# Zeros of the cache gradients: copied within memory from a first piece, in place of stores from a row on the chip

## The chip, the cores and the metric

The kernel runs on one core of a Trainium2 chip. The metric is the device time of one execution in microseconds (us); several executions are given by their median. A profile is one execution taken with the hardware profiler. Its span runs from the first to the last instruction; the execution's own time is a little longer.

## The reference

One token passes through two identical layers, each an attention over a window of a key/value cache followed by a dense block with the mish activation. The kernel returns the output and the gradients of all inputs.

```python
W = min(4096, max(256, Sk // 4))          # 4096 of Sk = 32768 positions
k = k_cache[:, :, Sk - W:, :]             # 4 groups of heads, 128 wide; v likewise
p = softmax(q @ k.T * Dh ** -0.5);  o = p @ v
x = x + attention(layernorm(x)) @ wo      # D = 1024, 32 heads
x = x + mish(layernorm(x) @ w1 + b1) @ w2 # F = 3584
# the same two lines once more with the same weights and caches;
# outputs: x and the vector-Jacobian product with grad_out
```

The gradients of the caches have the caches' full shape, (1, 4, 32768, 128) in bf16. Only the last 4096 positions took part, so the first 28,672 positions of each of the 4 groups of both caches have a gradient of zero. These zeros are 58.7 MB, and the kernel has to write them: about 60% of all that it writes.

## The kernel before, in words

The forward pass runs through attention, dense block, attention, dense block, and the backward pass returns through them in reverse. At the end come the weight gradients, which are outer products on TensorE.

Weights and cache windows are loaded by SyncE (SP) through `Ring` (L35 to L78), eight slots of 1 MB. `pump` (L68 issues the load) goes on in a fixed order as long as a slot is free, and `release` frees a slot once the work on it is queued. `W1`, `VS` and `KT` have places of their own. Attention weights pass through `EX`, the first half of `DSX`, and end in `PX` (first written at L530, in `attn_fwd`), which the backward pass reads at L805 and L958. The finished weight gradients and the window parts of the cache gradients leave through SP, too (`store`, L917), from stages that reuse `W1`, `VS`, `KT` and the ring.

The zeros are the filler of the schedule. A list, `zjobs`, holds 56 destinations of 1 MB: `out_2` and `out_3`, four groups each, seven pieces per group. A piece is 128 partitions by two rows of 4 KB (`ZC` = 2048 bf16). Each partition owns 224 rows of a cache group, 56 KB, so a piece is 128 stretches of 8 KB that lie 56 KB apart. All come from one tile of zeros, `zt`, 4 KB in each partition, which VectorE sets at the start (L168). `zeros(n, after)` (L237 to L243) first has GpSimd copy one element of `after` into `pz` (L238), so that GpSimd, which works in order, waits until that point of the computation. Then it issues the next `n` pieces from GpSimd's own DMA queue:

```python
nc.gpsimd.tensor_copy(pz[0:1, ...], after[0:1, 0:1])
...
nc.gpsimd.dma_start(dst, zt[:, None, :].to_broadcast([P, dst.shape[1], ZC]))
```

The calls are placed by hand: 6 pieces in the second attention's forward pass, 7 after it, 7 before the second dense block's backward pass, and then groups of 2 to 5 through the rest of the backward pass. GpSimd has little else to do: constants at the start, and small copies into `QC` (L470) and `DOC` (L785), whose second halves are read by TensorE late in the backward pass. ScalarE issues small DMAs, among them the three loads of inputs at the start (L196 to L198).

Of the kernel before, what the change touches and what calls it, by code (L numbers as in the profile page):

```python
# [10 lines left out]
BF16 = mybir.dt.bfloat16  # L11
# [4 lines left out]
P = 128  # L16
# [67 lines left out]
def kernel(  # L84
# [22 lines left out]
    nc = tc.nc  # L107
# [3 lines left out]
    ZR = Sk - W  # L111
# [7 lines left out]
    def sb(shape, dtype, name):  # L119
        return keep.tile(shape, dtype, name=name)  # L120
# [14 lines left out]
    PX = sb([P, 2 * 1024], BF16, "PX")  # L135
# [3 lines left out]
    gbc = DSX[:, 1024:2048]  # L139
    junk = sb([P, 1024], BF16, "junk")  # L140
    ZC = 2048
    zt = sb([P, ZC], BF16, "zt")


    SC = [psum.tile([P, 512], FP32, name=f"SC{i}")[:] for i in range(2)]
# [29 lines left out]
    for hi in range(4):  # L175
        r = slice(32 * hi, 32 * hi + 32)
# [47 lines left out]
    zjobs = []  # L224
    for out_t in (out_2, out_3):
        for g in range(G):
            dst = out_t[0, g, 0:ZR, :].rearrange("(p r) d -> p (r d)", p=P).rearrange("p (r c) -> p r c", c=ZC)
            for k in range(0, dst.shape[1], 2):
                zjobs.append(dst[:, k:k + 2, :])
    zjobs.reverse()  # L230

    pz = sb([1, 32], FP32, "pz")
    pz_n = [0]

    def zeros(n, after=None):

        if after is not None and zjobs:  # L237
            nc.gpsimd.tensor_copy(pz[0:1, pz_n[0]:pz_n[0] + 1], after[0:1, 0:1])  # L238
            pz_n[0] += 1
        for _ in range(n):  # L240
            if zjobs:
                dst = zjobs.pop()
                nc.gpsimd.dma_start(dst, zt[:, None, :].to_broadcast([P, dst.shape[1], ZC]))  # L243


    KEEP_Q = (6, 7)
# [452 lines left out]
    def wo_hook1(c):  # L699
        if c == 0:  # L700
            zeros(6, OC[:, 0, 1:2])
        conv(1)

    x3, st3, sA1 = attn_fwd(1, x2, st2, False, wo_hook1, last_da)
    zeros(7, x3)
    sB1 = mlp_fwd(1, x3, st3)
    conv(8, "A")
# [137 lines left out]
    nc.vector.tensor_tensor(out=dh1[:], in0=da1[:], in1=mp1[:], op=ALU.mult)  # L845
    nc.vector.tensor_copy(DHC[:, :, 1], dh1[:])
    zeros(7, dh1)
    g3 = dn_b1(g4)
    sB1["act_late"]()
# [224 lines left out]
```

## Time and profile before

| what | value |
|---|---|
| median of 3 runs | 479.27 us (478.96 to 480.3) |
| the profiled execution | 478.89 us, span 477.1 us |
| busy: TensorE, VectorE, ScalarE, GpSimd | 351.7, 277.9, 245.3, 45.2 us |
| moved by DMA | 183.41 MB, mean 384 GB/s |
| memory read, written | 83.90 MB, 98.58 MB |
| pieces of zeros | 56, issued from 137.5 to 378.0 us |
| from issue to landing of a piece | 4.8 / 13.0 / 24.5 us (least, median, most) |

A DMA is issued on the queue of an engine: q1 is SP's, q10 ScalarE's, q0 GpSimd's (`software_dynamic`), and q8 carries the fetches of instructions. All run on the same 16 DMA engines. A transfer is cut into packets, here one for each row. The share in the table of queues is the time that a queue's packets took, as a part of the 16 engines' time in that stretch; packets overlap slightly, so a full stretch reads a little over 100%. In a row of the stretches, "x" is the number of instructions. The chain of waits is followed back from the last instruction, at each step to what released it.

### The profile page before, as it was taken

The page shows a single profiled execution, that of the slowest core. Times are in us where ns is not written, and L with a number is a line of the kernel's source. Part 1 is how long each engine was busy: PE and PEld are TensorE (multiplying, and loading weights), DVE is VectorE, ACT ScalarE, POOL GpSimd, SP SyncE. Part 2 cuts the span into 40 slices and gives each one's busy share as a digit, 9 for nine tenths or more (in the row PEclk, how much of TensorE's full clock was granted, in tenths as well). Part 3 has the DMA queues.
Part 4 walks back from the last instruction along what each step waited for, and adds up shares of the span by engine and source line. Part 5 has one row for each costly group of instructions (what it writes and reads, how often), then busy time and mean ns, then how long its engine had stood idle before and what let it go on. Part 6 is the DMA issues. An engine that isn't in the chain of part 4 may idle for free.

```text
span 477.1 us, 13273 instructions
## 1 busy us (share of the span) xinstructions
PE 351.7 (74%) x5841; PEld 268.5 (56%) x5841; DVE 277.9 (58%) x597; ACT 245.3 (51%) x358; POOL 45.2 (9%) x83
## 2 busy tenths in 40 slices
PE   4846345696688895888886976688778689999930
PEld 3746335696588784877876975556456323333300
DVE  4405820561331268896598825466176889999920
ACT  2402001171145296792594633675267589999920
POOL 1000000000043130102201011002302200000000
PEclk9955555555555588797897555555555555555555
DMA  8999999999969999999999999678999999999997
GB/s 337 423 419 419 418 419 418 421 400 383 420 252 394 396 394 406 347 410 368 416 421 366 363 345 414 229 190 325 417 420 415 388 415 413 418 420 414 419 420 306
DMA packets 33992, 183.41 MB, mean 384 GB/s; under 512 B 4217, under 2 KB 4238, under 8 KB 20622
## 3 DMA queue, kind: packets, MB, share of 16 engines
q1 hardware_dynamic: 17280, 123.74, 64.5%
q0 software_dynamic: 15232, 58.72, 31.2%
q8 instruction: 45, 0.74, 0.6%
q10 hardware_dynamic: 1422, 0.10, 0.2%
q14 instruction: 13, 0.11, 0.1%
HBM read 83.90 MB, written 98.58 MB: 382 GB/s over the span
## 4 chain that ended last, share of the span: by engine, by line
PE 46%; DMA 19%; DVE 16%; issue 7%; ACT 6%; ACTq 2%; DVEq 0%; SPq 0%
DVE junk L399 10%; PE BIG L921 8%; PE BIG L421 8%; DMA ring<-in_A_wo_dram 6%; PE SC L921 5%; DMA ring<-in_A_wq_dram 4%; DMA W<-in_B_w_dram 4%; PE BIG L568 3%; ACT ring L282 3%; PE MV L634 3%; DMA out_dram<-W 3%; PE BIG L967 2%; PE TP L433 2%; PE MV L587 2%; ACTq L884 2%
## 5 line engine op out<-in xcount | busy, mean ns | idle before, releaser
L282 ACT COPY ring<-BIG 128x1024 bf16<-128x1024 bf16 x82 | 81.8, 1046 | 38.5 <-PE BIG L421 29.4
L399 DVE CUSTOM_DVE_ANT_0 junk<-ring,SC 128x1024 bf16<-128x1024 bf16 x62 | 75.5, 1217 | 6.1 <-PE SC L305 3.4
L421 PE MATMUL BIG<-ident_bf,ring 128*128 128x128 bf16 x656 | 71.0, 278 | 8.9 <-ACT ring L282 2.4
L921 PE MATMUL BIG<-W 2*128 2x512 bf16 x163 | 68.3, 586 | 7.5 <-ACT W L282 3.2
L421 PEld LDWEIGHTS <-ring 128*128 128x128 bf16 x656 | 57.4, 126 | 22.0 <-issue 21.0
L921 PEld LDWEIGHTS <-W 2*128 2x128 bf16 x240 | 20.2, 101 | 39.9 <-issue 35.3
L243 POOL DMA_DIRECT2D out_dram<-zt x56 | 40.2, 720 | 3.5 <-DMA out_dram<-zt 3.0
L282 ACT COPY KT<-BIG 128x1024 bf16<-128x1024 bf16 x22 | 21.8, 1015 | 31.5 <-PE BIG L568 29.6
L282 ACT CAST W<-BIG 128x512 bf16<-128x512 f32 x55 | 31.2, 595 | 11.5 <-PE BIG L921 9.3
L433 PEld LDWEIGHTS <-ring 128*128 128x128 bf16 x704 | 30.8, 107 | 11.2 <-ACT ring L282 6.3
L921 PE MATMUL SC<-W 2*128 2x512 bf16 x77 | 35.3, 584 | 0.4 <-ACT VS L282 0.4
L282 ACT COPY W<-BIG 128x1024 bf16<-128x1024 bf16 (+2 forms) x33 | 26.5, 908 | 17.2 <-PE BIG L727 14.8
L279 DVE CAST W<-BIG 128x512 bf16<-128x512 f32 x30 | 20.3, 686 | 20.8 <-PE BIG L921 13.4
L539 PE MATMUL MV<-OC,ring 128*128 128x1 bf16 x512 | 16.5, 166 | 13.0 <-DMA ring<-in_A_wo_dram 12.2
L587 PE MATMUL MV<-NB,W 128*128 128x1 bf16 x448 | 16.4, 172 | 10.0 <-DMA W<-in_B_w_dram 6.6
L539 PEld LDWEIGHTS <-ring 128*128 128x128 bf16 x512 | 15.9, 106 | 13.7 <-DMA ring<-in_A_wo_dram 12.8
L461 PE MATMUL MV<-NA,ring 128*128 128x1 bf16 x512 | 15.0, 165 | 10.6 <-DMA ring<-in_A_wq_dram 9.4
L399 DVE CUSTOM_DVE_ANT_0 junk<-ring,DSX 128x1024 bf16<-128x1024 bf16 x18 | 22.0, 1224 | 0.5
L587 PEld LDWEIGHTS <-W 128*128 128x128 bf16 x448 | 16.1, 118 | 10.7 <-DMA W<-in_B_w_dram 7.7
L399 DVE CUSTOM_DVE_ANT_0 junk<-ring,SC,dnp 128x1024 bf16<-128x1024 bf16 x16 | 20.5, 1281 | 0.6
L967 PEld LDWEIGHTS <-W 32*128 32x128 bf16 x128 | 9.6, 101 | 19.9 <-issue 18.3
L461 PEld LDWEIGHTS <-ring 128*128 128x128 bf16 x512 | 14.3, 103 | 11.2 <-DMA ring<-in_A_wq_dram 10.0
(253 smaller groups left out, 593.3 us busy)
## 6 DMA issues: line engine op xcount, KB each, us to landing
out_dram<-zt POOLq DMA_DIRECT2D x56, 1024.0 KB, 13.0
ring<-in_A_wq_dram SPq DMA_DIRECT2D x27, 1024.0 KB
ring<-in_A_wo_dram SPq DMA_DIRECT2D x24, 1024.0 KB
ring<-in_B_w_dram SPq DMA_DIRECT2D x14, 1024.0 KB
out_dram<-W SPq DMA_DIRECT2D x11, 1024.0 KB
W<-in_B_w_dram SPq DMA_DIRECT2D x8, 896.0 KB
out_dram<-KT SPq DMA_DIRECT2D x7, 1024.0 KB
out_dram<-ring SPq DMA_DIRECT2D x7, 1024.0 KB
```

What stands on the lines that cost most here:

```text
L243: nc.gpsimd.dma_start(dst, zt[:, None, :].to_broadcast([P, dst.shape[1], ZC]))
L279: nc.vector.tensor_copy(dst, src)
L282: nc.scalar.copy(dst, src)
L399: nc.vector.tensor_tensor_reduce(out=out, in0=a, in1=vec, scale=1.0, scalar=acc if i else 0.0, op0=ALU.mult, op1=ALU.add, accum_out=acc)
L421: nc.tensor.transpose(b[:, i * P:(i + 1) * P], block(w, i) if block else w[:, i * P:(i + 1) * P], ident_bf[:])
L433: nc.tensor.matmul(out, lhsT=w[:, i * P:(i + 1) * P], rhs=rhs_of(i), start=fresh[0], stop=last and i == n - 1, skip_group_check=True)
L461: nc.tensor.matmul(q_ps[:, h:h + 1], lhsT=ch[:, h * P:(h + 1) * P], rhs=NA[:, t, l:l + 1], start=(t == 0 and h == 0), stop=(t == TD - 1), ...
L539: nc.tensor.matmul(y_ps[:, dd:dd + 1], lhsT=ch[:, tt, dd * P:(dd + 1) * P], rhs=OC[:, h, l:l + 1], start=(h == 0 and dd == 0), stop=(h == ...
L568: nc.tensor.transpose(b[:, i * P:(i + 1) * P], T[:, g, 8 * b8 + i, :], ident_bf[:])
L587: nc.tensor.matmul(h_ps[:, fb:fb + 1], lhsT=f_block(W1[:, t], fb), rhs=NB[:, t, l:l + 1], start=(t == 0 and fb == 0), stop=(t == TD - 1), ...
L921: nc.tensor.matmul(b[:, 0:n], lhsT=ROWS[base:base + 2, lo:lo + P], rhs=ROWS[base:base + 2, ro:ro + n], start=True, stop=True, tile_positio ...
L967: nc.tensor.matmul(b[:, k * 256:(k + 1) * 256], lhsT=RT[32 * g:32 * g + 32, a, tp, :], rhs=YS[32 * g:32 * g + 32, :], start=True, stop=Tru ...
```

## The change

The destinations are cut differently: each piece is now 4096 consecutive rows of a cache, 1 MB, as 128 rows of 8 KB. The first piece (`zfirst`) is written at the start from the chip, by two DMAs of 0.5 MB on ScalarE's queue. They stand in the program after the loads of inputs and before the first load of the ring. The other 55 pieces are no longer sent from the chip. GpSimd issues each as a DMA from `zfirst` in memory to its place in memory, at the same calls of `zeros` as before (the last call finds three pieces in place of four). The row of zeros no longer has a tile of its own: `zt` is a view of `PX`, which is free until the first attention's weights are written to it.

```diff
     ZC = 2048
-    zt = sb([P, ZC], BF16, "zt")
+    zt = PX[:, 0:ZC]
...
     for out_t in (out_2, out_3):
         for g in range(G):
-            dst = out_t[0, g, 0:ZR, :].rearrange("(p r) d -> p (r d)", p=P).rearrange("p (r c) -> p r c", c=ZC)
-            for k in range(0, dst.shape[1], 2):
-                zjobs.append(dst[:, k:k + 2, :])
+            for k in range(0, ZR, 4096):
+                zjobs.append(out_t[0, g, k:k + 4096, :].rearrange("(p r) d -> p (r d)", p=P))
+
+    zfirst = zjobs.pop(0)
     zjobs.reverse()
+    for k in range(2):
+        nc.scalar.dma_start(zfirst[:, k * ZC:(k + 1) * ZC], zt[:])
...
             if zjobs:
                 dst = zjobs.pop()
-                nc.gpsimd.dma_start(dst, zt[:, None, :].to_broadcast([P, dst.shape[1], ZC]))
+                nc.gpsimd.dma_start(dst, zfirst)
```

## The prediction

> **What bounds the kernel now.** I read the page from the DMA side, because the change touches nothing but transfers. First the page's slices (40 of 11.9 us: TensorE, the DMA engines' busy share, the rate), its table of queues and its count of memory traffic:
>
> ```profile
> PE   4846345696688895888886976688778689999930
> DMA  8999999999969999999999999678999999999997
> GB/s 337 423 419 419 418 419 418 421 400 383 420 252 394 396 394 406 347 410 368 416 421 366 363 345 414 229 190 325 417 420 415 388 415 413 418 420 414 419 420 306
> ...
> q1 hardware_dynamic: 17280, 123.74, 64.5%
> q0 software_dynamic: 15232, 58.72, 31.2%
> q8 instruction: 45, 0.74, 0.6%
> ...
> HBM read 83.90 MB, written 98.58 MB: 382 GB/s over the span
> ```
>
> The DMA engines are full in nearly every slice. q0 is the queue of GpSimd, and its 58.72 MB are the zeros: 31.2% of the engines' time. The rate never passes 423 GB/s, and since nearly every byte now crosses memory once (read or written, never both), that is also the most memory traffic that the trace ever shows.
>
> Next the busy time by stretch, with columns from left to right: stretch, length, five engines, granted clock, DMA share, GB/s.
>
> ```profile
> 0.00:137.00 137.00, 82.82 (x2100) 78.05 (x2101) 55.47 (x154) 31.37 (x40) 2.18 (x13) 0.59 0.97 400
> 137.00:300.00 163.00, 132.55 (x2630) 124.10 (x2630) 101.92 (x239) 94.81 (x110) 30.03 (x49) 0.70 0.98 382
> 300.00:340.00 40.00, 31.46 (x509) 23.55 (x508) 20.87 (x39) 23.08 (x33) 3.33 (x7) 0.50 0.78 270
> 340.00:380.00 40.00, 30.39 (x296) 19.43 (x294) 26.35 (x42) 23.93 (x38) 9.70 (x16) 0.50 1.01 410
> 380.00:462.00 82.00, 74.47 (x313) 23.41 (x313) 73.28 (x126) 72.09 (x137) 0.00 (x0) 0.50 1.01 416
> ```
>
> All zeros are issued between 137 and 378 us. There the only DMA room is some 0.02 of 163 us and 0.22 of 40 us; after 340 there is none to the end. The chain of waits explains why this does not hurt today: from 190 to 300 us it is nearly all work of VectorE, TensorE and ScalarE, so the zeros fill DMA time that the chain is not waiting for. The chain's DMA pieces lie before the zeros (14.7 us for a wq load, 19.8 for a wo load) and once after 300 (12.0 us for an output store that shares the engines with zeros). The two limits run side by side: making the zeros cheaper buys little, making them dearer soon costs in full.
>
> Last, the queue tables of three stretches in which one kind of transfer runs alone: loads (20 to 100 us), zeros (150 to 185), output stores (400 to 440).
>
> ```profile
> q1 hardware_dynamic: 4728, 33.38, 100.6%
> ```
>
> ```profile
> q0 software_dynamic: 3565, 13.77, 101.3%
> ```
>
> ```profile
> q1 hardware_dynamic: 2367, 16.63, 100.7%
> ```
>
> Share times 16 engines times length, over KB, is a price in engine-ns per KB. Loads in mostly 8 KB rows: 1288 us over 32,600 KB, 39.5. Zeros in 4 KB rows: 567 us over 13,450 KB, 42.2. Stores in mostly 8 KB rows: 645 us over 16,240 KB, 39.7. As rates those are 419, 395 and 417 GB/s.
>
> **The change, part by part.**
>
> *The 55 copies.* 56 zero transfers of 1 MB become one first piece and 55 copies of it. Their 57.67 MB now cost 57.67 / 395 = 146.0 us of all 16 engines. A copy from memory to memory is not in this trace, so it is bounded.
>
> Lower end: the engine carries each byte through once, and a copy costs what an 8 KB store does. Then 57.67 / 417 = 138.3 us, 7.7 us less DMA work. A piece's rows also become one unbroken MB, which is how the output stores of that row lie. Row length and place cannot be worth more than this, and between 229 and 245 us the old zeros already cost only 40.4 (82.5% of 16 us on 16 engines over 5.35 MB).
>
> Upper end: the memory side is what a packet occupies, and a copy has two of them. Then a KB costs 39.5 + 39.7 = 79.2 ns, that is 209 GB/s, and the copies take 275.9 us, 129.9 more.
>
> A row between: the 45 instruction fetches on q8, the only other large packets of the trace: 0.6% of 7634 engine-us over 723 KB, 63 ns per KB, and 222 us for the copies, 76 more.
>
> I take the upper end. At the lower one, a stretch of copies alone would move 417 GB/s out of memory and 417 into it, 834 together, twice the largest slice of the trace; 209 each way makes 418, what every full slice shows. The Trainium skill, page DMA: Bandwidth & Descriptors, section Latency and other measured facts, has copies between memory tensors at 207 to 214 GB/s in each direction, which it calls full. That page's 214 would make 269.5 us of the copies, an estimate, and 590 us of the sum below.
>
> *Where the extra DMA work goes.* 129.9 us have to lie somewhere. The room from 137 on is 0.02 x 163 = 3.3 us and 0.22 x 40 = 8.8, so 12 are swallowed if a backlog is there to fill it, and it would be: 23 of the 56 pieces are issued by 194 us, in a stretch without loads, and at 209 GB/s these take 115 us in place of 61. The loads issued from 198 us on then meet a queue of copies. So the chain, now compute from 190 to 300, gets waits for `ring<-in_A_wq_dram` and `ring<-in_B_w_dram`, later for output stores. Loads and copies both come in 8 KB packets, where zeros had 4 KB. Engines that alternate between queues by packet would leave the loads a smaller part than today, which shifts waits but adds no work. Net +117.9.
>
> *The first piece.* It leaves at about 2 us from ScalarE's queue as two stores of 0.5 MB in 4 KB rows, 1.05 / 395 = 2.7 us of the engines ahead of or among the K and wq loads. DMA is full from about 2 us and the chain waits for wq and wo loads up to 69 us, so up to 2.7 us are lost there; they come back after 340, where the last group has three pieces in place of four. Bounds 0 and +2.7; taken at 0, since in a kernel with full DMA this only changes the order.
>
> *Work on ScalarE and VectorE.* The memset of 0.91 us stays on VectorE and only has another target. ScalarE gets two issues of 0.3 to 0.6 us (its rows for the input loads), held until that memset ends at 2.1 us. Queued behind them are a table load and `dummy`, now at 2.0 and 3.5 us; they move by some 1.5 us. ScalarE's next work that anyone needs starts at 9.8 us after 6.1 idle, which covers it; uncovered it would be 1.5 us.
>
> *The borrowed tile.* `PX` is first written at 50.1 us by L530. That write now also waits for the two stores, which were issued 48 us before; the longest landing of a zero piece today is 24.5 us. Cost nothing; if they were late, VectorE's part of the first attention would be.
>
> *GpSimd.* Its issues, 0.72 us each, may get cheaper with half as many rows, but GpSimd is busy 9% and the saving is worth nothing. It already waits twice, 3.0 us together, for older zeros to land before it may issue. With copies at 5 us each it waits much longer, and behind the waiting issue are the `pz` copies, which are only triggers, and the small copies into `DOC`. The one at 328.7 us is read by TensorE some 30 us later, with nothing else of GpSimd's on the way. I put nothing on it and up to 10 us in the range.
>
> **Sum.** The profiled execution took 478.89 us (span 477.1 and 1.8 around it), 0.4 under the median of 479.27. 478.9 + 129.9 - 12.1 = 596.7; forecast 597.
>
> **The rivals.**
>
> *Copies as cheap as stores: faster.* The engine's stream is the limit and a second memory side rides along. For it: loads and stores cost the same, 39.5 and 39.7, so neither side looks like the narrow one, and the trace cannot tell a common stream limit from a memory limit. Against it: 834 GB/s of traffic. The same page of the Trainium skill, section Where 436 GB/s comes from, has the ports of the on-chip memory as the bottleneck; by that rule a copy, which passes none of them, would be no dearer than a store. The place of the gain is small. From 137 to 300 the chain does not wait for DMA. After 329 us there are 16 pieces left, 16.8 MB, worth 16.8/395 - 16.8/417 = 2.2 us; with the first piece's 2.7 lost and returned, 478.9 - 2.2 = 476.7. If every cheaper piece counted, it is 471.2. It decides from a copy price below 42.2 ns per KB.
>
> *In between: slower, by less.* Copies hit a limit above 423 GB/s that the trace never reaches, or overlap partly with loads on the same engine. The q8 row is the only one of this kind: 478.9 + 76 - 12 = 543. Anything from 485 to 575 belongs here. The Trainium skill, page HBM Reference, gives 716 GB/s for a domain; at 358 each way the copies would take 161 us, an estimate, and the total would be some 482.
>
> *The change doesn't do what it says.* If each copy were held until the one before had landed, because it reads from the tensor that others write, or its rows did not spread over all engines, the copies would run one at a time. With some 5 us of transfer and as much again of latency, 55 of them take over 500 us where 240 are there: over 620 us. Today's pieces to one tensor are issued 0.72 us apart without a wait, which speaks against it.
>
> **How the numbers follow.** Doubled copies 0.48 (575 to 625, 597 likeliest), between 0.27 (480.5 to 575), as cheap as stores 0.20, of which 0.14 land more than 0.3% below (471 to 477.5) and 0.06 within it, one at a time 0.05. A change of 0.3%, 1.4 us, is about what a measurement here can tell from none. So faster 0.14, same 0.06, slower 0.80. The range 474 to 612 leaves out the best part of the cheap case (0.06), the top of the doubled one (0.08) and the last rival (0.05). The slower cases alone span 485 to 612.
>
> **What would show it.** Between 150 and 185 us only copies run, so that stretch's rate is the verdict: 209 GB/s for my forecast, about 257 for the q8 row, 417 or more for the faster rival. q0's share should rise from 31.2% of 477 us to some 47% of 595 with half as many data packets, and memory reads from 83.9 to 141.6 MB. The chain between 200 and 350 us should show DMA loads. The 300 to 340 stretch's idle DMA should be gone. I am wrong if that rate is near 400, or if the DMA engines stand partly idle while copies wait.

## The result and the profile after

The changed kernel takes 509.21 us (median of 4 runs) beside 479.12 for the kernel before; the ratio on record is 1.065 with a 95% interval of 1.058 to 1.0721, that is 28 to 35 us. It is slower, as forecast, by 30 us and not by 118. The total lies in the range, but the mechanism that gave the forecast is not the one at work. The profiled execution took 508.16 us, its span is 506.4.

First the page of the kernel after: the slices of the DMA engines (now 12.7 us each), the queues and the memory traffic.

```profile
DMA  8999999999899999899989996779992789999996
GB/s 325 425 421 415 420 420 419 418 368 421 361 334 333 333 334 333 298 412 400 399 344 414 363 424 211 245 252 407 360 369 95 263 329 407 424 426 426 424 426 287
...
q1 hardware_dynamic: 17280, 123.74, 60.7%
q0 software_dynamic: 1760, 57.68, 31.7%
...
HBM read 141.57 MB, written 98.58 MB: 474 GB/s over the span
```

The second number of q0 is the surprise. 1760 packets are 880 of data and 880 of 4 bytes, which by their number mark the end of a transfer; 57.68 MB in 880 are 64 KB (65,536 bytes) each, sixteen to a copy. Both ends of a copy are one unbroken MB, and its 128 rows of 8 KB have become 16 packets of 64 KB. The price comes from the same row: 31.7% of 16 x 506.4 us over 56,320 KB is 45.6 ns per KB. The forecast had 79.2. In the slices where copies run alone the rate stands still at 333 to 334 GB/s, and the queue table of 150 to 185 us says nearly the same:

```profile
q0 software_dynamic: 351, 11.54, 99.6%
```

With the few instruction fetches in that stretch it is 331 GB/s, where zeros from the chip had 395, and 209 was forecast. So the copies as such cost 2568 / 16 = 160.5 us of the engines in place of 146, about 14 more. The other half of the loss is idle time: the queues' shares add up to 93.8% of 506.4 us, 475.0, where before they made 96.6% of 477.1, 460.9. Work grew by 14.1, idle by 15.2 us.

The stretches show where that idle time lies (columns as before; the last two are DMA share and GB/s):

```profile
300.00:340.00 40.00, 27.10 (x299) 20.94 (x297) 23.06 (x47) 23.03 (x34) 1.15 (x3) 0.50 0.72 244
340.00:380.00 40.00, 15.83 (x312) 10.93 (x311) 7.31 (x17) 5.54 (x10) 4.84 (x12) 0.50 1.00 380
380.00:400.00 20.00, 18.07 (x178) 13.05 (x178) 16.09 (x26) 15.13 (x21) 2.10 (x5) 0.50 0.47 163
```

From 340 to 380 the DMA engines are full and the compute engines mostly stand: VectorE is busy 7.3 of 40 us, ScalarE 5.5. From 380 to 400 it is the reverse, and 0.53 of 20 us of DMA time goes unused. The chain of waits names the transfers in question (start, length, what):

```profile
253.95 27.10 DMA ring<-in_B_w_dram
291.62 19.98 DMA ring<-in_A_wo_dram
350.15 28.98 DMA out_dram<-W
```

In the chain before, the first two are absent, and the third was

```profile
335.47 12.00 DMA out_dram<-W
```

The moments at which GpSimd passes its `pz` triggers show how the delay builds up:

| trigger | before, us | after, us | later by |
|---|---|---|---|
| first zeros (`OC`) | 136.88 | 139.12 | 2.2 |
| end of the second dense block's backward (`g_B`) | 191.56 | 197.91 | 6.4 |
| second attention's backward (`DQC`) | 229.04 | 236.45 | 7.4 |
| inside the first dense block's backward (`dh`) | 280.35 | 292.05 | 11.7 |
| first attention's backward (`DQC`) | 339.87 | 355.69 | 15.8 |
| the next one (`dnp`) | 358.88 | 390.54 | 31.7 |
| end of the span | 477.1 | 506.4 | 29.3 |

About half of it arises in one step, where an output store waits for copies: from `DQC` to `dnp` it is 19.0 us before and 34.9 after.

The length of a wait in the chain is not its price, though. The wait of 27.10 us for a w2 load lies between the rows of the second attention's `DQC` and the first dense block's `dh`, and this stretch grew from 51.3 to 55.6 us. The chain went through compute there before, so most of the load's time ran beside work that had to be done anyway.

### The profile page after: what moved, and what is told of

Read it like the earlier page. It is cut to its first block, busy times and chain, and to the rows that moved or that the text cites. A ratio compares the mean times of both kernels' runs of the same rounds, so it can differ in the third digit from the quotient of the medians.

```text
span 506.4 us, 13276 instructions
## 1 busy us (share of the span) xinstructions
PE 352.5 (70%) x5841; PEld 269.4 (53%) x5841; DVE 278.0 (55%) x597; ACT 245.8 (49%) x358; POOL 31.8 (6%) x82
## 3 DMA queue, kind: packets, MB, share of 16 engines
q0 software_dynamic: 1760, 57.68, 31.7%
HBM read 141.57 MB, written 98.58 MB: 474 GB/s over the span
## 4 chain that ended last, share of the span: by engine, by line
PE 38%; DMA 35%; DVE 10%; ACT 7%; issue 5%; ACTq 1%; DVEq 0%; SPq 0%
DMA ring<-in_A_wo_dram 10%; PE BIG L925 8%; PE BIG L425 7%; DVE junk L403 6%; DMA out_dram<-W 6%; DMA ring<-in_B_w_dram 5%; PE SC L925 5%; ACT ring L286 4%; DMA ring<-in_A_wq_dram 4%; DMA VS<-in_A_v_cache_dram 4%; DMA W<-in_B_w_dram 3%; PE BIG L572 2%; PE BIG L971 2%; PE MV L591 2%; PE MV L638 2%
## 5 line engine op out<-in xcount | busy, mean ns | idle before, releaser
L925 PE MATMUL BIG<-W 2*128 2x512 bf16 x163 | 68.4, 585 | 18.6 <-DVE W L283 11.7
L403 DVE CUSTOM_DVE_ANT_0 junk<-ring,SC 128x1024 bf16<-128x1024 bf16 x62 | 75.5, 1218 | 10.3 <-DMA ring<-in_B_w_dram 4.5
L286 ACT CAST W<-BIG 128x512 bf16<-128x512 f32 x55 | 31.2, 595 | 23.6 <-PE BIG L925 21.5
L283 DVE CAST W<-BIG 128x512 bf16<-128x512 f32 x30 | 20.3, 687 | 39.7 <-DMA out_dram<-W 22.9
L286 ACT COPY KT<-BIG 128x1024 bf16<-128x1024 bf16 x22 | 21.8, 1015 | 33.8 <-PE BIG L572 31.7
L247 POOL DMA_DIRECT2D out_dram<-out_dram x55 | 26.7, 491 | 10.2 <-DMA out_dram<-out_dram 9.8
L591 PE MATMUL MV<-NB,W 128*128 128x1 bf16 x448 | 16.3, 172 | 12.1 <-DMA W<-in_B_w_dram 6.6
L465 PE MATMUL MV<-NA,ring 128*128 128x1 bf16 x512 | 15.2, 165 | 12.5 <-DMA ring<-in_A_wq_dram 11.7
L591 PEld LDWEIGHTS <-W 128*128 128x128 bf16 x448 | 16.0, 118 | 12.7 <-DMA W<-in_B_w_dram 7.3
```

The lines of the kernel that those rows point to most:

```text
L247: nc.gpsimd.dma_start(dst, zfirst)
L283: nc.vector.tensor_copy(dst, src)
L286: nc.scalar.copy(dst, src)
L403: nc.vector.tensor_tensor_reduce(out=out, in0=a, in1=vec, scale=1.0, scalar=acc if i else 0.0, op0=ALU.mult, op1=ALU.add, accum_out=acc)
L465: nc.tensor.matmul(q_ps[:, h:h + 1], lhsT=ch[:, h * P:(h + 1) * P], rhs=NA[:, t, l:l + 1], start=(t == 0 and h == 0), stop=(t == TD - 1), ...
L591: nc.tensor.matmul(h_ps[:, fb:fb + 1], lhsT=f_block(W1[:, t], fb), rhs=NB[:, t, l:l + 1], start=(t == 0 and fb == 0), stop=(t == TD - 1), ...
```

## The experiments

Two theories were set against each other. The packet theory: 64 KB packets hold the engines so long that loads and stores wait for their turn. The rate theory: copying within memory is slow, whatever its packets. In the first comparison (`first_only`, `copy8k`, `early64`, `late64`) the kernel before took 477.28 us. The edits are shortened; they are against the kernel after, those of `eight`, `chip2k` and `move4` against the kernel before.

**Only the first piece, from the chip otherwise (`first_only`).**

```diff
-    zt = PX[:, 0:ZC]
+    zt = sb([P, ZC], BF16, "zt")
...
-                nc.gpsimd.dma_start(dst, zfirst)
+                nc.gpsimd.dma_start(dst.rearrange("p (r c) -> p r c", c=ZC), zt[:, None, :].to_broadcast([P, 2, ZC]))
```

> The first piece leaves at the start on ScalarE's queue and pieces are unbroken MBs, as after the change, but the other 55 are stored from the chip in 4 KB rows, as before it. All theories: the changed kernel reached its first group of zeros 2.2 us later than the kernel before, which is the price of the first piece at the start. So 481 us (479.1 + 2.2), less up to 2.2 if the piece that is missing in the last group gives it back: 479 to 481.5. If the unbroken place of the pieces costs or saves something by itself, it shows here as a total outside of that.

Measured: 478.21 us, ratio 1.0015 (0.9993 to 1.0038), a little under the range. The first trigger comes at 139.23, 2.35 later than before, the last one at 378.99 is 3.35 later, and the span ends at 477.1 in both profiles: the cost at the start is real and is given back after the last trigger. That the piece missing there gives it back fits, and was not tested by itself. The unbroken place of the pieces changes nothing either: 393 GB/s between 150 and 185 us.

**Copies in packets of 8 KB (`copy8k`).**

```diff
+            dst = out_t[0, g, 0:ZR, :].rearrange("(p r) d -> p (r d)", p=P)
-            for k in range(0, ZR, 4096):
-                zjobs.append(out_t[0, g, k:k + 4096, :].rearrange("(p r) d -> p (r d)", p=P))
+            for k in range(0, dst.shape[1], 4096):
+                zjobs.append(dst[:, k:k + 4096])
```

> Copies within memory as after the change, but a piece is again 128 stretches of 8 KB that lie 56 KB apart, so a copy is 128 packets of 8 KB, not 16 of 64 KB. Packet theory (the loss comes from 64 KB packets, which hold the engines while loads and stores wait for their turn): the waits of 27 us for a w2 load and of 29 us for an output store go back to about 0 and 12, and the total is 479.1 + 2.2 for the first piece + 4 to 8 for the slower copies while they run alone = 485 to 490. Rate theory (the loss comes from the lower rate of copies, whatever their packets): 333 GB/s again between 150 and 185 us, the two waits stay, 505 to 512. Forecast on record (memory occupied twice): refuted already at 64 KB; if it held for 8 KB packets, 209 GB/s in that stretch and 590 or more.

Measured: 486.0 us, ratio 1.0197 (1.0148 to 1.0245). The queue of 150 to 185 us, and the chain:

```profile
q0 software_dynamic: 1564, 11.40, 97.9%
```

```profile
267.55 12.62 DMA ring<-in_B_w_dram
341.04 14.26 DMA out_dram<-W
```

The rate of copies alone is 328 GB/s, close to the 331 with 64 KB packets, yet the total is 23 us lower (509.21 against 486.0, across two comparisons) and the two waits of 27 and 29 us are 12.6 and 14.3. Packet size is most of the loss. The w2 wait was expected to vanish and did not. It does not measure the copies: `chip2k` below copies nothing, and its chain has a w2 wait of 10.3 us, while its `dh` trigger comes at 280.36, as in the kernel before (280.35). The step with the output store, from the first attention's `DQC` to `dnp` in the table of triggers, is the better measure: it takes 19.3 us in `first_only`, 21.9 here and 34.9 in the kernel after.

Where loads and copies share the engines (210 to 250 us) the engines move 424 GB/s, and the 400 of the kernel before there include a gap:

```profile
q1 hardware_dynamic: 1199, 8.77, 52.1%
q0 software_dynamic: 1115, 8.09, 48.2%
```

48.2% of 16 x 40 us over 8.09 MB is 39.0 ns per KB, the price of a store. In the stretch of copies alone the same working gives 49.2. Beside other transfers, a copy is not dear.

**64 KB copies early or late (`early64`, `late64`).** Each keeps a tile `zt` of its own and chooses by the number of pieces left (the comment stands for the second kernel).

```diff
-                nc.gpsimd.dma_start(dst, zfirst)
+                if len(zjobs) >= 33:          # early64; late64: len(zjobs) < 33
+                    nc.gpsimd.dma_start(dst, zfirst)
+                else:
+                    nc.gpsimd.dma_start(dst.rearrange("p (r c) -> p r c", c=ZC), zt[:, None, :].to_broadcast([P, 2, ZC]))
```

> Copies of 64 KB packets for the first 22 pieces after the first one, which run almost alone on the engines (137 to 206 us); the other 33 pieces are stored from the chip in 4 KB rows. Packet theory: no load or store waits behind those copies, so only the lower rate counts, 22 x 1.05 MB at 333 in place of 395 GB/s = 11 us of DMA work of which the compute beside it hides some: 479.1 + 2.2 + 4 to 8 = 485 to 489. Rate theory in its plain form (each copied MB costs alike): 22 of 55 copies give two fifths of 30 us, 491.

> The other way round: the first 22 pieces after the first one are stored from the chip in 4 KB rows, the last 33, which share the engines with loads and output stores, are copies of 64 KB packets. Packet theory: nearly the whole loss is here, 479.1 + 2.2 + 20 to 25 = 501 to 506, with the waits for the w2 load and for the output store near 27 and 29 us. Rate theory: three fifths of 30 us, 497, and those waits shorter in proportion.

Measured: early 482.41 us (ratio 1.0118, 1.0081 to 1.0154), late 500.43 (1.0503, 1.046 to 1.0546). Over `first_only` that is 4.2 us for 22 copies that run almost alone, and 22.2 for 33 that share the engines. Together with the first piece's 0.9 they make 27.3 of the 30 us, just under the whole's interval. The extra DMA work is nearly equal in both: q0's share comes to 154.4 us early and 154.7 late, beside 146.5 in `first_only`. So some 8 us of work cost 4 where hardly any load or store runs beside them, and 22 where loads and stores wait. The store's wait in the chain, late:

```profile
341.06 29.14 DMA out_dram<-W
```

With early copies it is 12.13. Both totals speak for packets and against an equal price for each copied MB. Both lie just under the ranges of the packet theory, which were added to 479.1 us and not to the 477.28 measured here; early lies under it even so, as the extra work was 8 us and not 11. In the late kernel's chain the expected w2 wait is absent; a wo load is awaited for 19.6 us there.

**Packets of 16 KB (`copy16k`).** In this comparison the kernel before took 477.78 us.

```diff
-            for k in range(0, ZR, 4096):
-                zjobs.append(out_t[0, g, k:k + 4096, :].rearrange("(p r) d -> p (r d)", p=P))
+            dst = out_t[0, g, 0:ZR, :].rearrange("(p r) d -> p (r d)", p=64)
+            for k in range(0, dst.shape[1], 8192):
+                zjobs.append(dst[:, k:k + 8192])
...
-    for k in range(2):
-        nc.scalar.dma_start(zfirst[:, k * ZC:(k + 1) * ZC], zt[:])
+    for k in range(4):
+        nc.scalar.dma_start(zfirst[:, k * ZC:(k + 1) * ZC], zt[0:64, :])
```

> As copy8k, but a piece is 64 stretches of 16 KB (112 KB apart), so a copy is 64 packets of 16 KB. Alternation theory (the engines take one packet of each queue in turn): while the two output stores of 1 MB after 340 us wait, 16 store packets of 0.31 us per engine each let one copy packet of 0.62 us pass, 14.8 us, and some 4 us pass before the first of them starts: a wait of 19 us, between the 14.3 of 8 KB and the 29 of 64 KB packets, and stores at half the rate of copies in that stretch. The wait for the w2 load, 12.6 with 8 KB and 27 with 64 KB packets, comes to 15 to 19. Total 490 to 496. If packet size matters only through some threshold between 8 and 64 KB, the waits are those of copy8k and the total is 486.

Measured: 493.67 us, ratio 1.0338 (1.0319 to 1.0358). The store's wait in the chain:

```profile
343.83 21.10 DMA out_dram<-W
```

It is 21, two more than expected, and the step from `DQC` to `dnp` takes 28.8 us, between 21.9 with 8 KB and 34.9 with 64 KB. The w2 wait is 11.8, below its range. The chain has a wait of 38.6 us for a wq load from 218 us on, which was not expected: the step it reaches into, from the second attention's `DQC` to `g_A`, takes 33.0 us beside 27.8 in `first_only` and 28.9 in the kernel after. Why this load suffers most with 16 KB packets stays open. The queue tables of the stretch in which stores and zeros compete show the turns: first `copy8k` from 346 to 358 us, then `copy16k` from 349 to 360, then the kernel after from 355 to 376.

```profile
q0 software_dynamic: 345, 2.54, 50.3%
q1 hardware_dynamic: 350, 2.53, 49.9%
```

```profile
q0 software_dynamic: 211, 2.75, 65.6%
q1 hardware_dynamic: 211, 1.50, 34.7%
```

```profile
q0 software_dynamic: 192, 6.29, 79.0%
q1 hardware_dynamic: 249, 1.72, 22.3%
```

With 8 KB packets both queues move the same bytes, with 16 KB the copies 1.8 times as many, with 64 KB 3.7 times. Turns of one packet each would give 1, 2 and 8. The first two fit. With 64 KB packets they do not: 96 packets of copies went by, and beside them 225 of stores (249 less those of 4 bytes), over two to each copy packet. A copy packet took 79.0% of 16 x 21 us / 96 = 2.8 us, so single turns would have made the store's 16 packets on each engine wait some 50 us, an estimate, where 29 were measured. Why more than one store packet passes for each copy packet there is not shown. What is shown is the share: stores had 22.3% of the engines' time and copies 79.0%.

The Trainium skill describes a round robin by packet on its page DMA: Bandwidth & Descriptors, in Queues, rings and completion order. The tables with 8 and 16 KB agree with it if one record of the trace is one turn; the table with 64 KB does not.

**Another MB for each copy (`copy8k_far`, timed once).**

```diff
+            far = (A_k_cache if out_t is out_2 else A_v_cache)[0, g, 0:ZR, :].rearrange("(p r) d -> p (r d)", p=P)
...
-                nc.gpsimd.dma_start(dst, zfirst)
+                dst, far = zjobs.pop()
+                nc.gpsimd.dma_start(dst, far)
```

> As copy8k, but every copy reads another MB, from the unused part of the input caches, so these outputs are not zeros. Is the lower rate of copies alone (328 GB/s) due to one MB being read again and again? If so, the stretch from 150 to 185 us shows clearly more than 328, up to 395 or 417. If it is a limit on reading and writing memory together, 320 to 335 again and the total is near copy8k's 486.

Measured: 326 GB/s between 150 and 185 us, 485.6 us in all. Reading one MB again and again is not the cause.

**Copies on eight engines (`eight`, timed once).**

```diff
+    def half(T, g):
+        return T[0, g, 0:ZR, :].rearrange("(p q r) d -> p q (r d)", p=8, q=28)
+    ejobs = [(half(out_2, g)[:, 0:16, k:k + 4096], half(A_k_cache, g)[:, 0:16, k:k + 4096])
+             for g in range(G) for k in range(0, 16384, 4096)]
...
+            if ejobs:
+                nc.scalar.dma_start(*ejobs.pop())
```

> A measurement, not a kernel: in the place of the first 16 pieces, 16 copies of 1 MB within memory are issued from ScalarE's queue, each as 8 rows of 16 parts of 8 KB, which should spread over 8 engines, not 16; they read from the unused part of an input, and most of out_2's zeros are left out. What limits copies that run alone to 328 GB/s, some 0.40 us for 8 KB on each of 16 engines? If it is the memory's total (328 read and 328 written), half as many engines stay below it and each packet takes 0.31 us, 212 GB/s from 8 engines. If each engine is slower at copying by itself, a packet still takes 0.40 us, 164 GB/s. The total time says nothing.

The queue table from 150 to 180 us, copies alone:

```profile
q10 hardware_dynamic: 830, 6.40, 50.5%
```

50.5% of 16 engines for 6.40 MB: half the engines are at work and move 213 GB/s, 38.8 ns per KB or 0.31 us for 8 KB. That is the price of a load or a store. An engine carries a copy as fast as anything else; only all sixteen together are held at some 330 GB/s. The queue differs too, ScalarE's in place of GpSimd's, but GpSimd's carried 395 GB/s of zeros. The whole run took 496.18 us, which says nothing, as most zeros of one output are left out.

328 read and 328 written are 656 GB/s. This fits a limit on the memory's total: beside loads, `copy8k` moved 8.77 MB one way and 8.09 MB both ways in 40 us, 624 GB/s of memory traffic, at the engines' full rate. That the limit lies in the memory, and not in something else that sixteen engines share, no run shows. The Trainium skill's page HBM Reference, section Specifications (TRN2), has some 716 GB/s for the domain, somewhat more than was measured.

**8 KB copies late only (`late8k`).** The kernel before took 478.04 us here. The edit is that of `late64` with the pieces of `copy8k`.

> As late64 (first 22 pieces from the chip, last 33 copied), but copies are 128 packets of 8 KB in pieces as before the change (56 KB apart). Alternation theory: beside loads and stores a copy of 8 KB packets costs what a store does (0.31 us a packet) and only takes one turn in two where 4 KB zeros took one third of the time: a store wait of about 14 in place of 12 us, a total of 478.2 (first_only) + 2 to 4 = 480 to 482. If copying within memory were dear by itself also while it shares the engines, 485 or more.

Measured: 483.5 us, ratio 1.0129 (1.0098 to 1.0159), above the expected 480 to 482 and below 485. The store waits 14.8 us, as expected, and the step from `DQC` to `dnp` takes 22.5 us beside 19.3 in `first_only`. That is 3 us of the loss. Another 3 lie after the last trigger, 101.1 us to the end in place of 98.1, and were not in the sum. The chain also has a w2 wait of 9.8 us, but from the second attention's `DQC` to `dh` this kernel takes 52.4 us and `first_only` 52.3, so it costs nothing. The turns explain the store's wait; the loss was put too low.

**Two attempts at a faster kernel.** Half the packet, from the chip (`chip2k`):

```diff
-    ZC = 2048
+    ZC = 1024
...
-            for k in range(0, dst.shape[1], 2):
-                zjobs.append(dst[:, k:k + 2, :])
+            for k in range(0, dst.shape[1], 4):
+                zjobs.append(dst[:, k:k + 4, :])
```

> The kernel before with zeros in packets of 2 KB, not 4 (half the row of zeros, twice the rows). Alternation theory turned round: the two output stores wait 4 us and then 16 x (0.31 + 0.08) = 6.3, some 10.3 in place of 12.0, and loads get four fifths of the engines in place of two thirds. Against it stands the price of smaller packets: if 2 KB cost 84 ns where 4 KB cost 159 to 165, the zeros cost 2 to 5% more, 3 to 7 us of DMA work, of which only the third that is issued after 329 us lies where DMA sets the end. Total 476 to 481, no clear change.

Measured: 481.42 us, ratio 1.0085 (1.0068 to 1.0102), slower by 0.85%. The profile's row of the zeros shows why it is no test of small packets:

```profile
q0 software_dynamic: 15232, 58.72, 32.3%
```

The number of packets is that of the kernel before; two rows of 2 KB travel as one packet of 4 KB and cost more (32.3% of 478.5 us against 31.2% of 477.1). The store waits 11.4 us.

And zeros into the idle stretch (`move4`), the kernel before with four pieces earlier:

```diff
     def dp1():
-        zeros(4, tmp([P, 64], FP32, "m641"))
...
+        if c in (1, 2, 3, 4):
+            zeros(1, tmp([P, HQ], FP32, "do32")[:, 4 * c:4 * c + 1])
```

> The kernel before, with the four pieces that were issued at 329 us, ahead of the output stores, issued one by one from about 300 us on, in the stretch from 300 to 340 us where DMA stands idle for 8.8 us. If DMA sets the end from 335 us on, four pieces fewer there are worth up to 10.6 us, limited by that room, less what the loads of that stretch lose: 470 to 475, and the wait for the output store falls from 12.0 to some 6 us. If the chain from there on is set by compute, 477 to 480.

Measured: 480.09 us, ratio 1.0051 (1.0035 to 1.0068): slower by 0.5%, and just above the 477 to 480 that were expected if compute sets the chain. The gain did not come. The wait for the output store is out of the chain, and the stretch is filled, but the chain and the stretches read:

```profile
301.29 8.05 DMA W<-W
```

```profile
300.00:340.00 40.00, 27.70 (x387) 19.88 (x385) 19.55 (x36) 22.70 (x33) 1.98 (x5) 0.50 0.94 288
340.00:380.00 40.00, 33.97 (x419) 22.84 (x416) 24.28 (x39) 23.64 (x38) 8.75 (x15) 0.50 0.89 355
```

DMA share rises from 0.78 to 0.94, TensorE falls from 31.5 to 27.7 us, and the share that was 1.01 afterwards is 0.89. The small transfers `W<-W` wait 8.05 us in place of 5.00, and the `DOC` copy comes at 332.27 in place of 328.69. This fits a stretch whose few transfers are all awaited; only the one wait was seen to grow. No version here beats the kernel before.

## Why the prediction was right and where it was wrong

*The step that failed* is the choice of the upper end for the copies: "a KB costs 39.5 + 39.7 = 79.2 ns". It measured 45.6, and the term of +129.9 us was worth +14. The reason given, that memory traffic would have to pass the 423 GB/s of the largest slice, took the most that the trace showed for the most that memory can do. But every transfer of that trace crosses memory once, and 16 packets of 8 KB in 0.31 us are 423 GB/s: it is what sixteen engines carry. The faster rival said that a second memory side rides along, and `eight` bears this out for a single engine. A limit above 423, which the rival in between asked for, exists too, at some 656 GB/s of traffic, and it was seen only while copies ran alone. The 207 to 214 GB/s that the Trainium skill has for copies (page DMA: Bandwidth & Descriptors, section Latency and other measured facts; it calls the 214 full) seemed to support the doubled price. It is not the rate here: sixteen engines made 321 to 334, and eight made 213.

*The second failing step* is "Loads and copies both come in 8 KB packets", and with it "shifts waits but adds no work". The packets were 64 KB, so a store got 22.3% of the engines' time where copies took 79.0%, and with 8 KB packets half. With DMA full I took every delay for a mere change of order. It was not: while stores waited, the compute engines stood, and when the copies were done, there was too little left to send; 15 us of DMA time went idle, and the 12.1 us of room that a backlog was to fill grew. That part was in no term of the sum, and it is half of the loss.

The two errors have opposite signs. With the measured 160.5 us in place of 275.9, the prediction's own sum gives 478.9 + 14.5 - 12.1 = 481.3. So the price made the forecast 115 us too high and the missing waits made it 28 too low. That the total lies in a range from 474 to 612 is therefore luck as far as the mechanism goes.

Of the prediction's own signs, the rate between 150 and 185 us was 331 and fitted neither 209 nor 417. q0's share was 31.7% and not 47%. The idle DMA time of the stretch from 300 to 340 us, which should have gone, grew from 0.22 to 0.28.

*What held.* The first piece costs 2.2 us on arrival at the first zeros and nothing in the end (`first_only`). ScalarE's table load moved from 2.04 to 3.09 us and nobody waited. `PX` was free in time. GpSimd's waits for older zeros grew from 3.0 to 9.8 us and nothing needed was seen to wait for it: the triggers and the copies into `DOC` were released by VectorE, not by older zeros. Memory reads rose to 141.57 MB, as said. The chain got waits for loads and for the output store after 200 us, as was said, though from turns and not from doubled work; they are for w2 and wo loads, and the expected one for wq is absent. The last rival, copies held one behind another, is out: six are issued within 3.05 us.

So the direction and, in the main, the places were right, the price of a copied KB was put 1.7 times too high, and what was missing was the length of a turn.

## What to carry to other kernels

A filler transfer is judged by the time one of its packets holds an engine, not only by its GB/s: between 8 and 64 KB packets at nearly the same rate lay 23 us of 480. To price a wait of the chain, compare the same two moments in both kernels: here one wait of 27 us stood for 4, and one of 29 for 16. Look at packet counts when both ends of a DMA are contiguous, since rows in the code need not be packets on the engines. And the largest rate in a trace is a limit only for the kind of traffic that the trace has; a few us of copies on half the engines tell a limit of each engine from one that all share.

## What the hardware showed that was not expected

- A copy with both ends unbroken ran as 16 packets of 64 KB per MB (880 for 55 copies); with pieces of 8 KB that lie 56 KB apart it was 128 per MB.
- Copies within memory: 0.31 us for 8 KB on eight engines (213 GB/s), but 321 to 334 GB/s on sixteen, with 8, 16 or 64 KB packets and from one source or many. Together with loads the engines moved 424 GB/s, and a copied KB cost 39.0 ns there in place of 49.2.
- Two queues shared the engines packet by packet with 8 KB against 8 KB and 16 KB against 8 KB; with 64 KB against 8 KB, 225 store packets passed beside 96 of copies.
- Rows of 2 KB, repeated from the chip, travelled two to a packet, and the zeros took 32.3% of the span's DMA time in place of 31.2%.
